# A gated MLP with seven-product block matmuls: sums of the down weights made in the first pass and kept in HBM, the other sums of the down stage on VectorE, fixed accumulator banks

## The chip, the cores and the metric

The kernel runs on one core of one Trainium2 chip. The metric is device time in microseconds (us) of that core, lower is better. The kernel before took 612.03 us (median of 4 runs, 611.32 to 613.72).

## The reference

```python
# x: 1 x 2048 x 1024, w_gate and w_up: 1024 x 3584, w_down: 3584 x 1024, all bf16
g = jnp.einsum("bsd,df->bsf", x, w_gate)
u = jnp.einsum("bsd,df->bsf", x, w_up)
h = jax.nn.gelu(g, approximate=True) * u
return jnp.einsum("bsf,fd->bsd", h, w_down)
```

## The kernel before

The kernel goes over x in two passes of 1024 rows. A pass has 14 "units" (gate and up for 256 columns of the hidden size, `u` = 0 to 13) and then one "down stage" (all of h times w_down). The first unit of the first pass is computed plainly while x is still being transposed, so units with seven products start at `u` = 1 there.

Every large product is cut into 2 x 2 blocks and computed with seven block products instead of eight. That saves one matmul in eight on TensorE and costs sums of blocks on the other engines: sums of weights ("s" in a unit, "t" in the down stage), sums of activations ("t" in a unit, "s" in the down stage), and additions of the seven products. A sum that goes into a matmul is written as fp32r, a 4-byte type.

```python
def dve(out, a, b, op):                       # L84
    nc.vector.tensor_tensor(out=out, in0=a, in1=b, op=op)
def pool(out, a, b, op):                      # L87
    nc.gpsimd.tensor_tensor(out=out, in0=a, in1=b, op=op)
def bank():                                   # 8 PSUM banks, handed out in turn
    return psum.tile([P, N], f32, name="bank")

def make_s(w):                                # sums of gate/up weights of one unit: 8 on GpSimd
    ...
    for i in range(2):
        s1.append(new(pool, a21, a22, ADD, "s1", sh))
    for i in range(2):
        s2.append(new(pool, s1[i], w[:, i, :KH, :P], SUB, "s2", sh))
    ...
def times(fb, c, g, u):                       # h = gelu(g) * u
    dve(hT[:, fb // NJ, fb % NJ, c, :], g, u, MUL)

def unit(u, xT, w, s, t, after_p5):
    ...                                       # seven products for gate (i=0) and up (i=1)
    c11 = [new(dve, c[i], p1[i], ADD, "sum", dtype=f32) for i in GU]
    ...
    times(2 * u, 0, gelu(c11[0]), c11[1])
    ...
    after_p5()                                # loads the next unit's weights, then make_s of them
    ...
    for i in GU:
        product(c[i], s4[i], tb, False)       # the product with s4 ("the fourth"): my mark
    ...
```

In the down stage the sums for products 5 and 6 (`prepare65`) and 7 and 3 (`prepare73`) are made just ahead of the matmuls that use them, for each of 14 values of `j`, partly on GpSimd:

```python
def prepare65(j):
    ra, rb = raw[j]                           # w_down, loaded again in each pass
    s1, t1, s2, t2 = q65[j] = pieces(j)
    dve(s1, hT[:, 0, j, 1, :], hT[:, 1, j, 1, :], ADD)
    pool(t1, ra[:, N:], ra[:, :N], SUB)
    dve(s2, s1, hT[:, 0, j, 0, :], SUB)
    dve(t2, rb[:, N:], t1, SUB)
    if j > 0:
        late4(j - 1)
    ...
def late4(j):
    eng = dve if j % 3 == 2 else pool
    q4[j] = new(eng, raw[j][1][:, :N], q65[j][3], SUB, "t4")
...
def prepare73(j):
    ...
    dve(s3, hT[:, 0, j, 0, :], hT[:, 0, j, 1, :], SUB)
    pool(t3, rr[:, 1, :], rr[:, 0, :], SUB)
    eng = pool if j % 2 == 1 else dve
    eng(sx, hT[:, 1, j, 0, :], hT[:, 1, j, 1, :], SUB)
    dve(s4, sx, s3, ADD)
...
def down(ip, last, next_x, next_ops):
    ...                                       # products 1 and 2 from plain h and w_down: 28 steps of 4 matmuls
    for i in I:                               # a finished quarter: added, cast, stored
        store(ip, 0, i, 0, lambda st: dve(st, c[i], p1[i], ADD))
    c = [bank() for _ in I]                   # the next accumulators: need those four to be out
    for t in range(NJ + LAG):
        ...                                   # products 6 and 5; then 3 and 7; then 4
```

So a down stage has 7 x 14 x 4 = 392 matmuls, and per `j` eight sums: `s1`, `s2`, `t1`, `t2`, `t4`, `s3`, `t3`, and `s4` with its helper `sx` (nine operations, 126 in a stage).

The start, in the order of the program: the first half of x is transposed on TensorE (`turn(xT, xn0, 0)`), then 32 plain matmuls, the weight sums for unit 1 (`make_s`), the second half of x (`turn(xT, xn1, 1)`), two products `times`, the 16 sums of x (`make_t`, all on VectorE), then 32 more plain matmuls and two more `times`.

## Time and profile before

| What, in the profiled run (span 610.5 us) | us |
|---|---|
| Start, up to the mark of unit 1 | 48.8 |
| Twelve units to the mark of unit 13 | 151.4 |
| First down stage (203.81 to 316.37) | 112.6 |
| Second down stage (497.36 to 607.20) | 109.8 |

Marks: I took the start of what I call the fourth product of a unit, the one with the weight sum `s4` (it is the sixth of the seven to run; in the trace, the group of matmuls that reads `tb` and `s`), since every unit has exactly one.

The page's slices: each digit is the busy share of one fortieth of the span in tenths, and PEclk is the granted TensorE clock in tenths.

```profile
PE   8659999999999994989698999999999999678977
...
DVE  1695665656555899998496766756566579999982
...
POOL 0956688877883467684446999888868437659640
PEclk9789999999999998899998999999999999969899
```

TensorE is at 9 except at the start (the first three digits) and in two stretches with lower digits, slices 16 to 22 and 35 to 40, which lie in the down stages and just behind the first. There VectorE shows mostly 8s and 9s, GpSimd is busy too, and the clock dips.

The stretch view of the two down stages (columns: stretch, length, then busy time and instructions of TensorE, TensorE's weight loads, VectorE, ScalarE and GpSimd; granted clock, DMA share, GB/s):

```profile
203.81:316.37 112.56, 94.53 (x390) 65.68 (x393) 100.06 (x107) 25.84 (x48) 67.10 (x46) 0.94 0.47 139
497.36:607.20 109.84, 93.99 (x390) 65.78 (x392) 95.42 (x97) 23.47 (x42) 65.26 (x43) 0.94 0.36 118
```

TensorE has 94.5 us of work in 112.6 us, some of that at a reduced clock. VectorE is busy for 100.1 us and GpSimd for 67.1 us at the same time. Memory is not what limits: the DMA engines are busy 47% of the time on average, and in this stage TensorE waits for no transfer. It idles 18.0 us: 8.9 for finished accumulators that VectorE has to store, 4.7 for sums of GpSimd and 4.1 for sums of VectorE.

In the timeline of TensorE the marks of units 2 and 3 are at 61.43 and 74.05 us: an undisturbed unit takes 12.62 us, and its matmuls follow each other without a wait. The units are bound by TensorE; there is little to gain there.

Why is VectorE so busy in the down stage? The timeline of VectorE in the first down stage of before (columns: start, length, engine, line, operation, tiles, shapes, count):

```profile
225.04 1.65 DVE L85 TENSOR_TENSOR q<-hT 128x512 fp32r<-128x512 bf16 x1
226.72 0.69 DVE L85 TENSOR_TENSOR q<-q,hT 128x512 fp32r<-128x512 f32 x1
227.33 0.68 DVE L85 TENSOR_TENSOR q<-raw,q 128x512 fp32r<-128x512 bf16 x1
...
228.54 1.65 DVE L85 TENSOR_TENSOR q<-hT 128x512 fp32r<-128x512 bf16 x1
230.22 1.53 DVE L85 TENSOR_TENSOR q<-q,hT 128x512 fp32r<-128x512 f32 x1
```

and the timeline of GpSimd in the same kernel and stretch:

```profile
222.97 3.18 POOL L88 TENSOR_TENSOR q<-raw 128x512 fp32r<-128x512 bf16 x2
228.10 1.54 POOL L88 TENSOR_TENSOR t<-raw,q 128x512 fp32r<-128x512 bf16 x1 [1.96 <-DVE q L85]
229.60 1.60 POOL L88 TENSOR_TENSOR q<-raw 128x512 fp32r<-128x512 bf16 x1
```

On VectorE, operations of the same shape take either 0.68 to 0.69 or 1.5 to 1.65 us. They are all sums of two operands in SBUF. GpSimd is in its own sums up to 226.15 and again from 228.10 to 231.20; the slow operations are the ones that fall into these times, and the fast ones fall between them. The Trainium skill states the reason (SBUF — State Buffer, "Who interferes with whom"): VectorE and GpSimd share one of their port pairs to SBUF, and "A DVE instruction with two SBUF inputs contends with a GpSimd instruction that reads SBUF, not with one that only writes it". The durations here agree with it: where GpSimd reads, a VectorE sum takes more than twice as long. The view of the tile `q` gives it for all sums of one form (minimum/median/maximum in ns):

```profile
L85 DVE TENSOR_TENSOR q<-hT x62: 674/1159/1658, 217.6 to 589.6; 128x512 fp32r<-128x512 bf16 x62
```

What this does to TensorE is seen in its timeline, where the bracket tells how long TensorE idled before the group and on whom it waited:

```profile
244.06 6.61 PE L106 MATMUL bank<-w 128*128 128x512 f32 x16 [8.94 <-DVE st L85]
250.51 11.72 PE L106 MATMUL bank<-q 128*128 128x512 f32 x51
```

TensorE waits 8.94 us until VectorE has added and stored four finished accumulators, since these additions stand in VectorE's queue behind slow sums. After the idle the next 16 matmuls take 6.61 us, 0.41 us each (the fp32r matmuls behind them start 0.227 us apart), at a granted clock of 0.50 in the stretch 240 to 250 us. The Trainium skill has this as well (TensorE: Matmul & The Clock Gate, "Part 1: The HAM clock gate"): the clock is halved after an idle window. So a wait costs more than its own length.

The start of before, in the timeline of TensorE:

```profile
45.48 3.48 PE L106 MATMUL bank<-t,s 128*128 128x512 f32 x8 [6.11 <-issue]
48.80 1.55 PE L106 MATMUL bank<-tb,s 128*128 128x512 f32 x6
```

Here there is a hole of 6.11 us inside unit 1. The trace names nobody that TensorE waited for (`issue`); I read the cause from what VectorE does. It is then working through the 16 sums of x, to 42.45 us; the first eleven of them take 1.3 to 1.66 us each, since GpSimd makes the weight sums at the same time.

### The profile page before, as it was taken

The page shows a single profiled execution, that of the slowest core. Times are in us where ns is not written, and L with a number is a line of the kernel's source. Part 1 is how long each engine was busy: PE and PEld are TensorE (multiplying, and loading weights), DVE is VectorE, ACT ScalarE, POOL GpSimd, SP SyncE. Part 2 cuts the span into 40 slices and gives each one's busy share as a digit, 9 for nine tenths or more (in the row PEclk, how much of TensorE's full clock was granted, in tenths as well). Part 3 has the DMA queues.
Part 4 walks back from the last instruction along what each step waited for, and adds up shares of the span by engine and source line. Part 5 has one row for each costly group of instructions (what it writes and reads, how often), then busy time and mean ns, then how long its engine had stood idle before and what let it go on. Part 6 is the DMA issues. An engine that isn't in the chain of part 4 may idle for free. (4 is left out here: it accounts for less than half of the span.)

```text
span 610.5 us, 7424 instructions
## 1 busy us (share of the span) xinstructions
PE 554.5 (91%) x2398; PEld 385.9 (63%) x2432; DVE 436.1 (71%) x501; ACT 248.4 (41%) x426; POOL 408.7 (67%) x312
## 2 busy tenths in 40 slices
PE   8659999999999994989698999999999999678977
PEld 4337766777667552867475777767777665366756
DVE  1695665656555899998496766756566579999982
ACT  2525555565555110141453555555555531003350
POOL 0956688877883467684446999888868437659640
PEclk9789999999999998899998999999999999969899
DMA  8354222342003951434446743222400196232312
GB/s 261 84 154 119 73 70 69 99 110 69 1 1 123 371 162 35 153 88 104 121 129 179 193 120 88 70 69 77 125 7 2 56 345 220 70 119 71 103 34 87
DMA packets 96133, 67.59 MB, mean 111 GB/s; under 512 B 12128, under 2 KB 87904, under 8 KB 96096
## 3 DMA queue, kind: packets, MB, share of 16 engines
q1 hardware_dynamic: 96096, 67.12, 37.5%
q8 instruction: 20, 0.33, 0.2%
q14 instruction: 17, 0.14, 0.1%
HBM read 60.82 MB, written 4.19 MB: 106 GB/s over the span
## 5 line engine op out<-in xcount | busy, mean ns | idle before, releaser
L88 POOL TENSOR_TENSOR s<-w 128x512 fp32r<-128x512 bf16 x108 | 137.6, 1293 | 90.1 <-PE bank L106 57.6
L106 PE MATMUL bank<-t,s 128*128 128x512 f32 x648 | 161.2, 404 | 8.7 <-issue 6.1
L106 PE MATMUL bank<-w 128*128 128x512 bf16 (+1 forms) x532 | 135.7, 401 | 26.2 <-DVE st L85 17.9
L85 DVE TENSOR_TENSOR sum<-bank,p 128x512 f32<-128x512 f32 x108 | 74.4, 691 | 103.3 <-PE bank L106 101.4
L106 PEld LDWEIGHTS bank<-t,s 128*128 128x128 f32 x648 | 123.4, 191 | 38.8 <-issue 7.6
L102 ACT COPY p<-bank 128x512 f32<-128x512 f32 x124 | 71.3, 589 | 80.5 <-PE bank L106 67.1
L85 DVE TENSOR_TENSOR hT<-g,sum 128x512 bf16<-128x512 f32 x81 | 82.6, 1020 | 12.9 <-ACT g L152 7.1
L88 POOL TENSOR_TENSOR q<-raw 128x512 fp32r<-128x512 bf16 x48 | 73.0, 1530 | 27.0 <-DMA raw<-in_w_down_dram 12.1
L152 ACT ACTIVATE g<-sum 128x512 f32<-128x512 f32 x81 | 51.2, 632 | 96.9 <-DVE sum L85 95.1
L106 PEld LDWEIGHTS <-w 128*128 128x128 bf16 x496 | 45.0, 99 | 68.0 <-issue 23.0
L106 PE MATMUL bank<-t,sa 128*128 128x512 f32 x328 | 84.1, 404 | 0.0
L106 PE MATMUL bank<-q 128*128 128x512 f32 x272 | 69.3, 401 | 15.1 <-DVE q L85 10.1
L88 POOL TENSOR_TENSOR s<-w,s 128x512 fp32r<-128x512 bf16 x54 | 74.8, 1404 | 0.0
L106 PEld LDWEIGHTS bank<-t,sa 128*128 128x128 f32 x328 | 61.7, 188 | 14.8
L85 DVE TENSOR_TENSOR q<-hT 128x512 fp32r<-128x512 bf16 x62 | 71.0, 1163 | 0.0
L106 PEld LDWEIGHTS bank<-q 128*128 128x128 f32 x272 | 50.6, 190 | 30.5 <-POOL q L88 16.5
L88 POOL TENSOR_TENSOR s<-s,w 128x512 fp32r<-128x512 f32 x54 | 65.4, 1230 | 0.0
L97 ACT CAST tb<-raw 128x512 fp32r<-128x512 bf16 x28 | 17.2, 625 | 115.1 <-PE bank L106 78.1
L106 PE MATMUL bank<-tb,s 128*128 128x512 f32 x216 | 53.3, 389 | 0.0
L106 PE MATMUL bank<-raw,hT 128*128 128x512 bf16 x218 | 49.4, 379 | 0.3
L106 PEld LDWEIGHTS bank<-tb,s 128*128 128x128 f32 x216 | 40.5, 188 | 8.5
L102 ACT COPY u<-bank 128x512 f32<-128x512 f32 x62 | 35.7, 588 | 18.0 <-PE bank L106 17.8
(43 smaller groups left out, 463.3 us busy)
## 6 DMA issues: line engine op xcount, KB each, us to landing
raw<-in_w_down_dram SPq DMA_DIRECT2D x112, 256.0 KB, 5.3
w<-in_w_gate_dram SPq DMA_DIRECT2D x27, 512.0 KB, 4.0
w<-in_w_up_dram SPq DMA_DIRECT2D x27, 512.0 KB, 5.3
out_dram<-st SPq DMA_DIRECT2D x32, 128.0 KB, 1.7
xn<-in_x_dram SPq DMA_DIRECT2D x8, 256.0 KB, 4.4
w<-in_w_gate_dram SPq DMA_DIRECT2D x4, 128.0 KB, 4.1
w<-in_w_up_dram SPq DMA_DIRECT2D x4, 128.0 KB, 4.2
w<-in_x_dram SPq DMA_TRANSPOSE x16, 2.9
```

What stands on the lines that cost most here:

```text
L85: nc.vector.tensor_tensor(out=out, in0=a, in1=b, op=op)
L88: nc.gpsimd.tensor_tensor(out=out, in0=a, in1=b, op=op)
L97: nc.scalar.copy(out=t, in_=src)
L102: nc.scalar.copy(out=t, in_=ps)
L106: nc.tensor.matmul(ps, lhsT=lhs, rhs=rhs, start=start, stop=stop, skip_group_check=True)
L152: nc.scalar.activation(g, src, ACT.Gelu_apprx_tanh)
```

## The change

The intent was to take GpSimd out of the down stages and to make the down stage's weight sums (`t1`, `t2`, `t4`, 42 operations) only once: VectorE makes them in the units of the first pass, where it has time, they go to HBM as fp32, and each down stage loads them. Of the sums that stay, all are on VectorE, and `s4` is now made from `s2`, without the helper `sx`: five sums per `j`, 70 in a stage. The accumulators get fixed banks. To have room, the kernel holds fewer weight tiles and loads the weights of a unit one unit earlier. The additions in a unit write one of their results in place in PSUM, so the product of `times` reads PSUM and not two SBUF operands. Not shown below: in the first down stage the loads of x for the next pass start at once, and the sums for that pass's first unit are made inside the stage, all on VectorE; the last four accumulators of a stage are copied out by ScalarE alone.

```diff
-    def bank():
-        return psum.tile([P, N], f32, name="bank")
+    bank = [psum.tile([P, N], f32, name=f"bank{i}") for i in range(8)]
+    even, odd, cc, dd = bank[0:2], bank[2:4], bank[4:6], bank[6:8]
 ...
-    def make_s(w):
+    def make_s(w, eng):                 # unit 1 and unit 0 of pass 2: dve; all others: pool
 ...
+        def add(ps, other):
+            g = new(dve, ps[0], other[0], ADD, "sum", dtype=f32)
+            dve(ps[1], ps[1], other[1], ADD)
+            return g, ps[1]
 ...
+    td = dpool.tile([P, NJ, 3, N], f32, name="td")         # in HBM
+    def keep(j, part):                                      # called in a unit of the first pass
+        ra, rb = wraw[j]
+        if part == 0:
+            made[j] = mpool.tile([P, 3, N], f32r, name="m") # a single buffer
+            dve(made[j][:, 0], ra[:, N:], ra[:, :N], SUB)
+        elif part == 1:
+            dve(made[j][:, 1], rb[:, N:], made[j][:, 0], SUB)
+        else:
+            dve(made[j][:, 2], rb[:, :N], made[j][:, 1], SUB)
+    def store_made(j):
+        nc.sync.dma_start(out=td[:, j], in_=made[j].bitcast(f32))
 ...
+    def make12(j):                                          # for prepare65
+        dve(s1, hT[:, 0, j, 1, :], hT[:, 1, j, 1, :], ADD)
+        dve(s2, s1, hT[:, 0, j, 0, :], SUB)
 ...
+    def make73(j):                                          # for prepare73
+        dve(s3, hT[:, 0, j, 0, :], hT[:, 0, j, 1, :], SUB)
+        dve(t3, rr[:, 1, :], rr[:, 0, :], SUB)
+        dve(s4, hT[:, 1, j, 0, :], s12[j][1], SUB)
 ...
-    s = make_s(w)
+    s = make_s(w, dve)                                      # the start
     turn(xT, xn1, 1)
 ...
-    ps = [bank() for _ in JI]
+    ps = bank[0:2] + bank[6:8]
 ...
+    def making(u):                                          # which j in which unit
+        return {1: [0], 2: [1, 2], 3: [3], 4: [4, 5]}.get(u, [u + 1] if 4 < u < NU - 1 else [])
+    fetch_wd(0)
+    ahead = load_w(2)
 ...
             def prepare():
-                    nxt["w"] = load_w(u + 1)
-                    nxt["s"] = make_s(nxt["w"])
+                nxt["w"], nxt["s"] = ahead, None
+                if u + 1 < NU:
+                    nxt["s"] = make_s(ahead, pool)
+                if u + 2 < NU:
+                    ahead = load_w(u + 2)
```

## The prediction

> **What bounds it now.** The stretch view gives TensorE 150.2 of 150.9 us busy in gate/up units 2 to 13 of the first pass, 12.61 us a unit in the timeline: TensorE-bound. Losses are elsewhere:
>
> - Start: unit 1 ends at 52.9 us. TensorE waits 5.3 us for transposed x and 6.1 us in unit 1, for sums slowed to 1.6 us.
> - First down stage: 203.8 to 316.4, 112.6 us. At the undisturbed rates of the timeline (0.213 us per bf16, 0.227 to 0.233 per fp32r matmul) its 392 matmuls need about 88.5.
> - First unit of pass 2: 18.6 instead of 12.6 us.
> - Second down stage: 497.4 to 607.2, 109.8 us.
>
> In the down stages VectorE is 95 to 99% busy for 65 us, and TensorE's largest wait (8.9 us each) is for four stores queued behind VectorE's sums. A VectorE sum of two SBUF operands takes 0.68 us alone but 1.5 to 1.65 beside a GpSimd sum; GpSimd's go from 1.13 to 1.6. The Trainium skill (SBUF — State Buffer, "Who interferes with whom") says that a two-input VectorE instruction contends with GpSimd's reads; the trace agrees. Two engines blocking each other bound the stage. The idle also costs clock: the 16 matmuls after it take 0.41 us each.
>
> **What the change does.**
> 1. Down stage: GpSimd's 40-odd sums go away; VectorE keeps 70 sums and 8 stores, 78 x 0.68 = 53 us of 88.
> 2. Weight sums, once: 42 VectorE operations in pass 1, three per unit, six in units 2 and 4, 0.7 to 1.6 us each. VectorE's load goes from about 7.5 to 10.5 of 12.6 us per unit (products now read PSUM: 0.68 instead of 1.02 us). Single units hide it; double ones stall 1 to 2 us each.
> 3. DMA: 11 MB written once; each down stage reads 11 MB of fp32 sums for 7.3 MB of raw bf16. Its first 28 steps (24 us) move as much as before (370 to 399 GB/s in the trace), but the first stage also gets the 16 x transposes there, about 10 us of engine time: 0 to 4 us of TensorE wait.
> 4. Start: unit 1's sums at 0.62 us on VectorE; x copies 1 us later; no 6.1 us hole, no cold restart.
> 5. Fixed banks: no cost.
>
> **Sum.** Start -8; pass-1 units +4; first down stage -20 (to 92.5); first unit of pass 2 -5; second down stage -18.5 (to 91). Together -47.5: 612 becomes **565 us**, 8 in 10 between **555 and 583**. Chances: faster by over 2% 0.95, within 2% 0.04, slower 0.01.
>
> **What would show each step right.** Unit 2 starts near 45 us. Units stay at 12.6 us, but up to 14.5 in units 2 to 5. In the down stages VectorE sums average under 0.75 us, VectorE is busy under 75%, GpSimd idle; no TensorE wait over 3 us; granted clock 0.97 or more; 89 to 95 us each. TensorE busy about 97%.
>
> **What would make it wrong.** (a) Down stages DMA-bound: TensorE waiting for w_down or stored sums, DMA share near 1 beyond the first 25 us, worse in the first. (b) The 52 slots run out (28 held by sums of h), loads issue late and the in-order queue stalls. (c) Pass-1 sums delay the PSUM sums: units of 13 us or more throughout. (d) VectorE waits for the single buffer of finished sums to reach HBM. Each would cost 5 to 20 us.

## The result

The kernel after took 560.05 us (median of 4 runs, 559.93 to 560.38), against 612.03 for before over its four runs. The ratio is 0.9148, with a 95% interval of 0.9129 to 0.9167. Ratios here are the mean time of one kernel's runs over that of the other's of the same rounds, so they are not quite the ratio of the medians. The mean granted clock went from 0.964 to 0.990. All outputs are right.

With the marks of the two traces, the 51.9 us between the spans (610.5 and 558.6) split into the terms of the prediction:

| Term | Before | After | Difference | Predicted |
|---|---|---|---|---|
| Start to the mark of unit 1 | 48.80 | 46.27 | -2.5 | -8 |
| Unit 1 to unit 13 of pass 1 | 151.38 | 152.50 | +1.1 | +4 |
| First down stage | 112.56 | 87.74 | -24.8 | -20 |
| Rest, up to the mark of unit 0 of pass 2 | 16.99 | 12.98 | -4.0 | -5 |
| Unit 0 to unit 13 of pass 2 | 164.00 | 163.54 | -0.5 | 0 |
| From there to the end (second down stage) | 116.77 | 95.57 | -21.2 | -18.5 |

The slices of the page of after:

```profile
PE   5969999999999999999999999999999999999997
...
DVE  1797978788777778388695545555545548757730
...
POOL 0433596998788100000048766677777700000000
PEclk9998999999999999999999999999999999999999
```

TensorE's only low digits are now at the start (and the last slice, where the kernel ends). GpSimd is all but idle in the down stages, and the clock is at 9 from the fifth slice on. The stretch view of the two down stages of after:

```profile
202.40:290.14 87.74, 87.58 (x390) 63.29 (x393) 67.60 (x106) 26.15 (x47) 3.33 (x3) 1.00 0.86 247
466.66:555.25 88.59, 88.22 (x390) 63.24 (x392) 52.38 (x84) 24.01 (x43) 0.00 (x0) 1.00 0.56 183
```

TensorE is busy for 87.58 of 87.74 us and 88.22 of 88.59 us, at full clock. The DMA share in the first stage is 0.86, because the stored sums and the transposed x come in together, but TensorE doesn't wait for them. VectorE's busy time fell from 100.1 to 67.6 and from 95.4 to 52.4 us. In the first stage that includes the 24 sums for the next pass's first unit, which is why the count there is 106.

VectorE's timeline in the first down stage of after, where the same group of four stores is found as in the wait of before:

```profile
227.61 2.48 DVE L90 TENSOR_TENSOR st<-bank,p 128x512 bf16<-128x512 f32 x4 [5.53 <-PE bank L111]
230.01 0.68 DVE L90 TENSOR_TENSOR q<-hT 128x512 fp32r<-128x512 bf16 x1
...
232.98 0.68 DVE L90 TENSOR_TENSOR q<-hT,q 128x512 fp32r<-128x512 bf16 x1
```

The four stores (2.48 us) now start when TensorE is done: VectorE waits 5.53 us for TensorE, and not the other way round. Every sum that the stage needs takes 0.68 or 0.69 us (two sums of the next pass's x, at its end, take 1.65 beside GpSimd). The view of the tile `q` for the form shown of before:

```profile
L90 DVE TENSOR_TENSOR q<-hT x56: 680/686/694, 203.3 to 525.5; 128x512 fp32r<-128x512 bf16 x56
```

The one large term that failed is the start. The timeline of TensorE in after:

```profile
11.96 0.95 PE L399 MATMUL bank<-ident,xn 128*128 128x128 bf16 x8 [4.79 <-DMA xn<-in_x_dram]
...
14.93 7.36 PE L111 MATMUL bank<-xT,w 128*128 128x512 bf16 x31
...
40.99 5.45 PE L111 MATMUL bank<-t,s 128*128 128x512 f32 x12 [4.41 <-DVE hT L90]
46.27 2.02 PE L111 MATMUL bank<-tb,s 128*128 128x512 f32 x8
```

There are a wait of 4.79 us for x at 11.96, before the first plain matmul, and a wait of 4.41 us for `hT` at 40.99. The matmuls after the second one run at 0.45 us each, at a granted clock of 0.50 (40.99 to 46.27). In VectorE's timeline the wait is explained:

```profile
31.22 1.65 DVE L90 TENSOR_TENSOR t<-xT,xT 128x512 fp32r<-128x512 bf16 x1
32.90 0.69 DVE L90 TENSOR_TENSOR t<-xT,t 128x512 fp32r<-128x512 bf16 x1
...
37.24 2.49 DVE L90 TENSOR_TENSOR t<-xT,t 128x512 fp32r<-128x512 bf16 x4
39.65 1.28 DVE L90 TENSOR_TENSOR hT<-g,bank 128x512 bf16<-128x512 f32 x2
```

The last two products of the start (39.65, `hT<-g,bank`, which free banks 6 and 7 for unit 1) stand behind all 16 sums of x, and the first five of these (25.12 to 32.87) take 1.48 to 1.65 us and not 0.69. GpSimd's timeline tells what ran beside them:

```profile
20.91 2.91 POOL L93 TENSOR_TENSOR s<-w 128x512 fp32r<-128x512 bf16 x2 [19.61 <-DMA w<-in_w_gate_dram]
...
29.14 3.18 POOL L93 TENSOR_TENSOR s<-w,s 128x512 fp32r<-128x512 bf16 x2
```

These are the weight sums of unit 2, from 20.91 to 32.32 us. In before they came from 26.33 to 38.89, behind those of unit 1. The change took unit 1's sums off GpSimd, and unit 2's, with their weights now loaded a unit earlier, moved up into the gap.

### The profile page after: what moved, and what is told of

Same layout as the page of the kernel before. It is cut to its first block, busy times and chain, and to the rows that moved or that the text cites. A ratio compares the mean times of both kernels' runs of the same rounds, so it can differ in the third digit from the quotient of the medians.

```text
span 558.6 us, 7422 instructions
## 1 busy us (share of the span) xinstructions
PE 541.4 (97%) x2398; PEld 381.1 (68%) x2432; DVE 367.7 (66%) x533; ACT 247.5 (44%) x430; POOL 242.6 (43%) x206
## 4 chain that ended last, share of the span: by engine, by line
PE 89%; DMA 4%; DVE 4%; issue 1%; ACT 1%; SPq 0%; DVEq 0%; ACTq 0%
PE bank L111 88%; DMA td<-m 2%; DVE m L90 2%; DMA xn<-in_x_dram 2%; DVE hT L90 1%; DVE t L90 1%; ACT g L157 0%; DVE sum L90 0%; PE bank L399 0%; SPq L391 0%; DVE xT L402 0%; ACT sa L102 0%; ACT st L362 0%; ACT u L107 0%; SPq L411 0%
## 5 line engine op out<-in xcount | busy, mean ns | idle before, releaser
L93 POOL TENSOR_TENSOR s<-w 128x512 fp32r<-128x512 bf16 x100 | 122.7, 1246 | 203.5 <-DVE t L90 103.0
L111 PE MATMUL bank<-xT,w 128*128 128x512 bf16 x468 | 111.6, 380 | 2.1 <-DVE xT L402 0.2
L90 DVE TENSOR_TENSOR hT<-g,bank 128x512 bf16<-128x512 f32 x112 | 76.7, 687 | 18.6 <-PE bank L111 8.5
L90 DVE TENSOR_TENSOR sum<-bank,p 128x512 f32<-128x512 f32 x54 | 37.2, 688 | 72.4 <-PE bank L111 72.3
L93 POOL TENSOR_TENSOR s<-w,s 128x512 fp32r<-128x512 bf16 x50 | 61.8, 1260 | 0.0
L111 PE MATMUL bank<-q 128*128 128x512 f32 x240 | 59.1, 389 | 0.0
L111 PE MATMUL bank<-t,sa 128*128 128x512 f32 x216 | 58.6, 413 | 0.0
L111 PEld LDWEIGHTS bank<-t,sa 128*128 128x128 f32 x216 | 40.7, 188 | 10.5
L90 DVE TENSOR_TENSOR q<-hT 128x512 fp32r<-128x512 bf16 x56 | 38.4, 687 | 10.3 <-PE bank L111 9.1
L90 DVE TENSOR_TENSOR bank<-bank,p 128x512 f32<-128x512 f32 x54 | 37.6, 696 | 8.3 <-PE bank L111 6.9
```

The source lines that it names most:

```text
L111: nc.tensor.matmul(ps, lhsT=lhs, rhs=rhs, start=start, stop=stop, skip_group_check=True)
```

## The experiments

Three theories of the large gain were open after this:

- A (mine): two engines collide. VectorE's sums of two SBUF operands and GpSimd's sums block each other. Taking GpSimd's sums out of the down stage is the gain.
- B: fewer sums. The sums of weights are made once and `sx` is saved; collisions matter little.
- C: the fixed banks. Order or hand-over of accumulators was what made TensorE wait.

And two theories of the missing part at the start: D, the collision of GpSimd's early unit-2 sums with the sums of x; and E, the order of TensorE's instructions (the wait for x at 11.96). The order of the instructions shows that the scheduler put 24 of the 32 transposes of the second half of x ahead of the first plain matmul in after, and behind it in before.

Each kernel ran four times (the last one five), beside before on the same chip. The groups of runs that share a chip are e1 to e4 (before: 612.99), e5 to e8 (613.42) and e9 to e12 (614.28).

### e1_all_vector: before, with all sums of the down stage on VectorE

```diff
-        pool(t1, ra[:, N:], ra[:, :N], SUB)
+        dve(t1, ra[:, N:], ra[:, :N], SUB)
 ...
-        eng = dve if j % 3 == 2 else pool
+        eng = dve                                  # late4: t4
 ...
-        pool(t3, rr[:, 1, :], rr[:, 0, :], SUB)
-        eng = pool if j % 2 == 1 else dve
+        dve(t3, rr[:, 1, :], rr[:, 0, :], SUB)
+        eng = dve                                  # sx
```

> The kernel before with the GpSimd sums of the down stage moved to VectorE and nothing else; VectorE then does 126 sums and 12 stores per down stage where it did about 85 and 12. Theory (the two engines block each other): its two-operand sums fall from a mean of about 1.1 us to 0.68, one every 0.61 us, and each down stage gets some 10 us shorter in spite of the added sums: 585 to 603 us in all; the wait for the four stores stays near 9 to 12 us. Rival (the number of sums binds, not the collisions): 126 sums at the old 1.1 us fill about 139 us, and the time rises above 640 us.

Measured: 583.83 us, ratio 0.952 (0.9474 to 0.9566). VectorE now does all 126 sums of a stage, nothing is saved, and the kernel is 29 us faster. The view of the tile `q` in this kernel, and the stretch view of the first 378 recorded matmuls of its first down stage:

```profile
L85 DVE TENSOR_TENSOR q<-hT x76: 679/685/689, 215.9 to 560.0; 128x512 fp32r<-128x512 bf16 x76
```

```profile
203.57:297.60 94.03, 89.12 (x378) 62.18 (x381) 91.28 (x150) 24.12 (x44) 0.00 (x0) 0.96 0.56 163
```

The sums, these and those of the other forms, are all at 0.68 to 0.70 us. The stage, up to the next pass's first matmul at 300.47, takes 96.9 us instead of 112.6. Over the whole stage VectorE's instructions went up from 107 to 153, and their busy time went down from 100.1 to 94.2 us. One part of what I expected missed: I thought that the 8.9 us waits for the stores would stay, because VectorE would be 97% busy. They are gone; the largest waits of TensorE on VectorE in this kernel are 1.4 us. That is theory A without any saving, and it gives more than half of the whole gain (29 of 52 us). The remaining 24 us belong to the rest of the change. By the marks of the two profiled runs (578.8 and 558.6 us), 15.9 of the 20.2 us between them lie in the two down stages, where VectorE is still busy for 97% of the stretch in this kernel. That taking sums off VectorE gives these 15.9 us is likely but not shown alone, since the loads and the order of the stage change too.

### e2_banks_only: before, with the fixed banks of after

```diff
-    def bank():
-        return psum.tile([P, N], f32, name="bank")
+    bank = [psum.tile([P, N], f32, name=f"bank{i}") for i in range(8)]
+    even, odd, cc, dd = bank[0:2], bank[2:4], bank[4:6], bank[6:8]
 ...
-        e = [bank(), bank()]
+        e, c, d = banks                            # in unit; likewise in down, turn and the start
```

> The kernel before with fixed accumulator banks and nothing else. Theory: the 8.9 us waits for the four stores come from the stores standing behind VectorE's sums, not from how banks are handed out, so both waits remain and the down stages stay at 110 to 113 us; the instruction order shows 24 transposes of the second half of x moved ahead of the first plain products on TensorE, so the first plain products start near 15 us instead of 8.3, and the total is 610 to 622 us. Rival (fixed banks take the waits away): the two waits vanish and the time falls to about 590 us.

Measured: 613.7 us, ratio 1.0016 (0.9976 to 1.0056), the same. The two waits of 8.9 us stay. Theory C falls. This kernel also has the transposes moved ahead, as after has, so that order comes with the fixed banks; why the scheduler does it then was not looked into further.

### e3_dummy_sums: after, with 42 useless GpSimd sums in each down stage

```diff
     def make12(j):
         s1, s2 = s12[j] = [slot([P, N], f32r, "q") for _ in range(2)]
+        for _ in range(3):
+            pool(warm, hT[:, 0, j, 1, :], hT[:, 1, j, 1, :], ADD)
```

> The changed kernel with 42 useless GpSimd sums per down stage, two SBUF operands each, into an unused tile. VectorE's work, the loads and the banks are unchanged. Theory (collisions): while they run VectorE's two-operand sums rise from 0.68 to a mean of 1.3 us or more, 28 of them no longer fit into the 24 us of the first two products, TensorE waits again for the stores, and the time rises by 15 to 50 us over the 560 us of the changed kernel. Rival (GpSimd was slow only with its own work, and its sums were late): the dummy sums harm nothing, 559 to 562 us.

Nobody uses what these sums write, so they add no dependence that the stage needs. Measured: 592.57 us, ratio 0.9668 (0.9624 to 0.9713), 32 us slower than after. GpSimd has nothing else to do there and runs the first stage's sums in one go, from 194.58 to 245.31, across the part of the stage ahead of the four stores. Beside them VectorE's sums take 1.5 to 1.65 us again (and 0.68 from 248.17 on), and TensorE again waits for the four stores. From VectorE's timeline, then TensorE's:

```profile
222.48 1.53 DVE L90 TENSOR_TENSOR q<-q,hT 128x512 fp32r<-128x512 f32 x1
223.94 1.64 DVE L90 TENSOR_TENSOR q<-hT 128x512 fp32r<-128x512 bf16 x1
```

```profile
246.51 5.39 PE L111 MATMUL bank<-w,q 128*128 128x512 f32 x16 [13.42 <-DVE st L90]
```

A wait of 13.42 us, and 14.1 us in the second stage; together 27.5 of the 32 us. Most of the rest is the slower clock after each wait: the 16 matmuls behind the two waits take 5.39 and 6.29 us, 0.34 and 0.39 us each where 0.23 is usual, about 4.4 us more. VectorE's own work is that of after. Theory B can't explain this; A does.

### e4_dummy_memset: after, with 84 GpSimd writes in each down stage

```diff
     def make12(j):
         s1, s2 = s12[j] = [slot([P, N], f32r, "q") for _ in range(2)]
+        for _ in range(6):
+            nc.gpsimd.memset(warm, 0.0)
```

> The same with 84 GpSimd memsets per down stage in place of the 42 sums: GpSimd is busy but reads nothing. Theory, with the Trainium skill (SBUF — State Buffer, Who interferes with whom): an instruction that only writes does not collide with a two-input VectorE sum, so the sums stay at 0.68 us and the time at 559 to 562 us. Rival (any GpSimd work at the same time slows VectorE): as with the dummy sums, in proportion to the time in which GpSimd is busy.

Measured: 559.69 us, ratio 0.9135 (0.91 to 0.917), no different from after. The groups view of this kernel (count, then busy time and mean ns):

```profile
L257 POOL MEMSET warm<- 128x512 bf16 x168 | 88.1, 524 | 9.6
```

GpSimd is busy with them for 44 us per stage, and the sums that VectorE makes meanwhile stay at 0.68 to 0.69 us. So it is not GpSimd being busy that costs, but GpSimd reading SBUF. This is what the sentence of the Trainium skill quoted above says, and here it is measured.

### e5_each_pass: after, with the weight sums made and stored in both passes

```diff
-            js = making(u) if ip == 0 else []
+            js = making(u)
 ...
-                for j in making(u + 1) if ip == 0 else []:
+                for j in making(u + 1):
 ...
-            if ip == 0 and making(u - 1):
+            if u > 0 and making(u - 1):
```

> The changed kernel, but the sums of the down weights are made in the gate/up units of both passes and stored twice, so nothing is made once. Theory: what matters is that they are out of the down stage; in a unit VectorE has room. In the changed kernel the first pass's units lost about 1 us against before (152.5 for 151.4 us), so the second pass loses about 1 us too: 560.5 to 563 us. Rival (having half as many of these sums gives the gain): 5 us slower or more.

Measured: 561.6 us, ratio 0.916 (0.9111 to 0.9208), 1.5 us over after, which is inside the noise (the intervals overlap). Making the sums once is not the gain; having them made outside the down stage is. In the units VectorE has the time.

### e6_back28: after, with 28 of the 70 sums of a stage back on GpSimd

```diff
-        dve(s3, hT[:, 0, j, 0, :], hT[:, 0, j, 1, :], SUB)
-        dve(t3, rr[:, 1, :], rr[:, 0, :], SUB)
+        pool(s3, hT[:, 0, j, 0, :], hT[:, 0, j, 1, :], SUB)
+        pool(t3, rr[:, 1, :], rr[:, 0, :], SUB)
```

> The changed kernel with 28 of the 70 sums of each down stage (the difference of h and the difference of w_down of the third product) back on GpSimd. Theory: collisions stretch VectorE's 14 remaining sums there and GpSimd's 28 take 1.2 to 1.6 us each, about 40 us in a window of about 45, so the slack nearly closes: 560 to 568 us, VectorE sums near 1 us in the second half of the stage. Rival (all sums must be on VectorE for any of the gain): over 575 us.

Measured: 566.0 us, ratio 0.9232 (0.9183 to 0.9281), 6 us over after. The view of the tile `q` shows the collisions:

```profile
L90 DVE TENSOR_TENSOR q<-hT,q x28: 681/1572/1651, 228.9 to 528.8; 128x512 fp32r<-128x512 bf16 x28
```

The sums collide (median 1572 ns) but TensorE hardly waits in the stages: they take 88.4 and 89.8 us, and the only waits in them are 1.5 us for stored sums, in the second. VectorE is busy for 72% of the first stage and 51% of the second here (73.4 us of 202 to 304, 47.3 of 468 to 560), so there is slack for it. By the marks, 3.3 of the 4.7 us between the profiled spans (563.3 and 558.6) lie behind the first stage, up to the mark of unit 0 of pass 2, where TensorE waits 2.02 us for ScalarE at 299.36; 1.3 lie between the last mark and the end. So a collision costs TensorE little where VectorE has slack: from 227.8 to 290 us of this kernel, where nearly all of the first stage's collisions fall, VectorE is busy for 68%. Before's VectorE was busy for 89% of the first stage, and for 99% of its first 40 us. Load and place were not varied apart: nearly all of GpSimd's sums here fall behind the four stores, and those of e3 ahead of them.

### e7_start_pool and e12_start_pool2: after, with GpSimd's unit-2 sums held back

```diff
             def prepare():
                 nonlocal ahead
                 nxt["w"], nxt["s"] = ahead, None
+                if ip == 0 and u == 1:
+                    pool(warm, t[3][KH - 1], t[3][KH - 1], ADD)
```

One small GpSimd sum reads the last sum of x, so everything behind it in GpSimd's queue has to wait until VectorE is done with the sums of x. e12 is the same kernel run again in the last group.

> The changed kernel with one small GpSimd sum that reads the last of VectorE's sums of x, ahead of GpSimd's weight sums for unit 2, which therefore start only after them. Theory: at the start GpSimd's sums for unit 2, now loaded a unit early, collide with VectorE's 16 sums of x (six of them at 1.5 to 1.65 us); without that the last one ends near 35 instead of 39.7 us, the two products behind it end near 36, TensorE's 4.4 us wait falls below 1 us, and the time is 554 to 557 us. Rival (the wait comes from something else in the start): no change, 559.5 to 561.

> The kernel with only GpSimd's weight sums for unit 2 held back, again, to be compared with the fully ordered start on the same chip: 552.5 to 554 us, as before.

Measured: e7 553.27 us, ratio 0.9019 (0.8969 to 0.9069); e12 553.56 us, ratio 0.9005 (0.8984 to 0.9025). That is 6.5 to 7 us faster than after. From e7's timelines of VectorE, GpSimd and TensorE:

```profile
33.87 1.28 DVE L90 TENSOR_TENSOR hT<-g,bank 128x512 bf16<-128x512 f32 x2
```

```profile
34.12 1.04 POOL L93 TENSOR_TENSOR warm<-t 128x512 bf16<-128x512 f32 x1 [32.81 <-DVE t L90]
```

```profile
36.95 2.11 PE L111 MATMUL bank<-t,s 128*128 128x512 f32 x8 [0.46 <-ACT u L107]
38.90 1.99 PE L111 MATMUL bank<-tb,s 128*128 128x512 f32 x8
```

The sums of x all take 0.69 us or less and end at 33.96 us, and not at 39.73, the wait for `hT` is gone (0.46 us are left, for ScalarE), and the mark of unit 1 is at 38.90 instead of 46.27. (In after's trace five sums of x are slow, not the six of the expectation.) The wait for x is still there (3.96 us at 11.46). Theory D is shown, and the 7.4 us gained at the mark are more than the 5.5 us that the prediction had missed at the start.

### e10_start_order: after, with the transposes of the second half of x back behind the plain matmuls

```diff
-    turn(xT, xn1, 1)
+    with tc.issue_after(held["mm"].ins):       # held["mm"]: the last plain matmul of the first half
+        turn(xT, xn1, 1)
```

> The changed kernel with only the TensorE order restored: the transposes of the second half of x behind the first plain products. Theory: the first products start near 8.5 instead of 15 us, but the copies of the second half of x stand behind the weight sums on VectorE until near 23 us, so the time saved turns into a wait there: 559 to 561 us. Rival (the moved transposes cost their 6 us): 553 to 556.

Measured: 560.01 us, ratio 0.9108 (0.9087 to 0.9129), the same as after. TensorE's timeline in this kernel:

```profile
7.40 7.07 PE L111 MATMUL bank<-xT,w 128*128 128x512 bf16 x32 [1.10 <-ACT xT L404]
...
21.01 12.38 PE L111 MATMUL bank<-xT,w 128*128 128x512 bf16 x48 [4.76 <-ACT g L157]
...
41.40 4.66 PE L111 MATMUL bank<-t,s 128*128 128x512 f32 x12 [4.40 <-DVE hT L90]
```

The first plain matmul starts at 7.40 and not at 14.93 us, but the time is given back: a wait of 4.76 us has appeared at 21.01, for ScalarE's gelu, which stands in its queue behind casts of unit 1's weights. VectorE's queue, which sets the pace here, hardly moved: its copies of the second half of x stand behind the sums of unit 1's weights, at 22.17 as against 22.73 us in after, and the products that TensorE waits for come at 40.07 as against 39.65. Theory E falls: the wait at 11.96 is visible and costs nothing as long as VectorE's queue sets the pace.

### e11_start_times: after, with two of the products moved ahead of the last four sums of x

```diff
-    t = make_t(xT)
     ps = bank[0:2] + bank[6:8]
-    for p, (j, i) in zip(ps, JI):
-        plain(p, i, j, 1, range(NKB))
-    for j in range(2):
-        times(j, 1, gelu(ps[2 * j]), ps[2 * j + 1])
+    def between():                              # called in make_t ahead of the four t4
+        for p, (j, i) in zip(ps, JI):
+            plain(p, i, j, 1, range(NKB))
+        for j in range(2):
+            times(j, 1, gelu(ps[2 * j]), ps[2 * j + 1])
+    t = make_t(xT, between)
```

> The changed kernel with only the two products of the second plain set moved ahead of the last four sums of x, GpSimd's collisions left as they are. Theory: TensorE waits in unit 1 for these products, through the fixed banks; they come four sums (2.4 us) earlier, so the time is 557 to 558.5 us. Rival (the wait is for the sums of x themselves): 559.5 to 561.

Measured: 559.24 us, ratio 0.9092 (0.9066 to 0.9119). That is under 1 us better than after, less than I expected, and I call it inconclusive. TensorE resumes at 39.02 and not at 41.40 us, but its fourth product starts at 45.97, as against 45.89 in e10: unit 1's first additions on VectorE come at 41.29 all the same, behind the last sums of x, and TensorE's next products need what follows from them.

### e8_start_all: e7, e10 and e11 together

The edits of the three together; the copies of the transposes are also placed ahead of the weight sums of unit 1:

```diff
+    with tc.issue_after(held["mm"].ins):
+        turn(xT, xn1, 1)
     s = make_s(w, dve)
-    turn(xT, xn1, 1)
 ...
+    t = make_t(xT, between)                     # as in e11
 ...
+                if ip == 0 and u == 1:          # as in e7
+                    pool(warm, t[3][KH - 1], t[3][KH - 1], ADD)
```

> The changed kernel with the start put in order: transposes of the second half of x held behind the first plain products on TensorE, their copies ahead of the weight sums on VectorE, the two products ahead of the last four sums of x, and GpSimd's sums for unit 2 behind all of them. Theory: the first plain products start near 8.5 us, the second near 18 instead of 24, the fourth product of unit 1 starts near 38 instead of 46.3 us: 550 to 554 us. Rival (the loads at the start bind): no better than 557.

Measured: 553.29 us, ratio 0.9016 (0.8973 to 0.9059), no better than e7 alone. TensorE starts its plain matmuls at 8.35 but waits 3.74 us for `hT` at 32.47, since the products now stand behind 12 sums of x, and the mark of unit 1 is at 39.97.

### e9_start_best: e8, with the products after the first four sums of x and the last four sums in unit 1

```diff
             t2.append(new(dve, b22, t1[k], SUB, "t2"))
+            if k == 1:
+                between()
 ...
+        def rest():
+            for k in range(KH):
+                t4.append(new(dve, xT[0][:, KH + k], t2[k], SUB, "t4"))
 ...                                            # in unit 1, after its first additions:
+        held.pop("rest", lambda: None)()
```

> The start of the previous run (everything in order) with two more moves on VectorE: the two products that free the second pair of banks come after four of the sums of x instead of after twelve, and the last four sums of x come after unit 1's first sums of products. Theory: in the previous run TensorE waited 3.7 us for those two products although their operands were ready near 25 us; without that the fourth product of unit 1 starts near 36 us instead of 40.0, and the time is 549 to 551.5 us, 2 us or more below the run with only GpSimd held back. Rival (the start is bound by the count of VectorE's sums, wherever they stand): no better than 552.5.

Measured: 554.47 us, ratio 0.9015 (0.8994 to 0.9035), against 553.56 for e12 in the same group. The mark of unit 1 came to 35.90 us, as I had meant, 2.6 us ahead of e12. But the time, which I had expected at 549 to 551.5, didn't fall. TensorE's timeline of this kernel in units 2 and 3:

```profile
48.37 1.98 PE L111 MATMUL bank<-tb,s 128*128 128x512 f32 x8
...
53.88 2.11 PE L111 MATMUL bank<-t,sa 128*128 128x512 f32 x8 [1.57 <-DVE sum L90]
...
57.70 3.88 PE L111 MATMUL bank<-t,s 128*128 128x512 f32 x16 [0.82 <-POOL s L93]
...
64.38 1.98 PE L111 MATMUL bank<-tb,s 128*128 128x512 f32 x8
```

From the mark of unit 2 to that of unit 3 are 16.0 us; in e12 they are 12.0 (51.88 to 63.87). The gain is lost to three waits, for VectorE, GpSimd and, at 62.48, ScalarE (0.90 us). VectorE's new sums of down weights in unit 2 had waited 3.17 us for the single buffer `m` to be stored, and then took 1.45 us, and 3.09 for the next two, beside GpSimd's sums of unit weights. When TensorE is ready sooner, the next limit is the other engines' work that the change has put there.

## Why the prediction was right or wrong

**The time was right.** 565 us was predicted, 560.05 measured, inside the range of 555 to 583, and "faster by over 2%" holds. That it came so near is in part luck: the start gave 5.5 us less and the first unit of pass 2 1 us less than the sum had, while the two stages gave 4.8 and 2.7 us more and the units of pass 1 cost 2.9 us less.

**The mechanism of the down stages was right.** The prediction said that two engines blocking each other bound the stage. e1 (same sums, all on one engine: -29 us), e3 (useless sums that read: +32 us) and e4 (useless writes: 0) show it. e2 and e5 take out the rivals: the banks, and making the sums once.

**Their size was too small.** I gave 92.5 and 91 us to the two stages (-20 and -18.5); they took 87.7 and 88.6 (-24.8 and -21.2). The 88.5 us that I had worked out for 392 undisturbed matmuls was about right (in the trace 112 bf16 matmuls at 0.216 us and 280 fp32r ones at 0.227 make 87.8 us), and the 2.5 to 4 us that I added for DMA waits were not needed: TensorE's waits for the stored sums in the first stage are 0, in spite of a DMA share of 0.86. I predicted VectorE under 75% busy; it was 77% in the first stage (67.6 of 87.7 us) and 59% in the second. The 24 sums for the next unit explain the first, and I had counted 8 stores where VectorE has 12.

**Pass-1 units: +4 predicted, +1.1 measured.** The units 2 to 5 of after take 13.41, 11.99, 13.37 and 12.73 us between marks, but a changed order of the matmuls moves the marks: in sum they are 51.5 against 50.47 us. The only stall that TensorE's timeline shows there is 0.48 us. VectorE's new sums do collide with GpSimd's weight sums in the units (first of each three: median 1.45 us), but the units have the slack for it: VectorE is busy for 9.8 us of a unit of about 12.5, where before had 7.6 and the prediction 10.5. The warning (d) did come true in itself, without harm: VectorE waited 16.6 us in 11 times for the single buffer of finished sums, but TensorE didn't have to.

**First unit of pass 2: -5 predicted, -4.0 measured.** No experiment took this term apart.

**The step that failed is item 4, "Start: unit 1's sums at 0.62 us on VectorE; x copies 1 us later; no 6.1 us hole, no cold restart", with its term "Start -8".** It measured -2.5. Unit 1 was to be over near 45 us, and its last product ends near 52.6. The hole did not go away; it became one of 4.4 us on `hT`, with a cold restart behind it. I had looked at what the change takes from GpSimd at the start (unit 1's sums) and not at what stands next in GpSimd's queue: the sums of unit 2, which moved from 26.33 up to 20.91 us and ran beside the sums of x in the place of unit 1's. It is the very collision that the prediction names as the limit of the down stages, half taken away and half left. The first sum of x started 2.7 us later than in before (25.12 against 22.46), behind VectorE's copies of x, which came 6.8 us later and not 1 (22.73 against 15.89); with five slow sums in place of eleven the last one ended 2.7 us sooner (39.73 against 42.45), and the mark came 2.5 us sooner. e7 takes it away with one dependence and gets 7 us back. The second thing that the traces showed at the start, the moved transposes with a wait of 4.79 us, looked the more striking and is worth nothing (e10).

**What points further.** e12 (and e7) beat both kernels: 553.56 against 614.28 us for before in the same group. The start isn't exhausted, but e8 and e9 gained nothing over them by a further change of VectorE's order, and e9 lost its lead in units 2 and 3. Whether spreading GpSimd's and VectorE's sums over those units would keep it was not tried.

## What to carry to other kernels

Two engines that share a port to SBUF are not two engines: here a VectorE sum of two SBUF operands took more than twice its time when GpSimd read beside it. First try to put all the work on one of them, even if the count of that one goes up. When a change takes work off an engine, look at what stands next in that engine's queue: it moves up into the gap, and may collide there just as well. The largest wait in a timeline can be worth nothing when another queue sets the pace, so take it away alone once before believing in it.

## What the Trainium skill lacked or had wrong

- SBUF — State Buffer ("Who interferes with whom") is right about who collides, and e4 agrees with its exception for operations that only write. It gives no durations for colliding sums of two tensors. Here a VectorE sum of two 128x512 operands goes from 0.68 or 0.69 to 1.5 to 1.65 us beside GpSimd's sums. GpSimd's own, of the same form, go from 1.15 us (before, at 17.64) to 1.59 us (before, at 26.33).
- The same page ("Summary: rules for kernel authors") says that the second one to issue fully blocks until the first finishes. The trace shows operations that last longer, not waiting ones: the lost time is inside the duration of the instruction (1.65 us), so in a profile the engine looks busy. The page doesn't say that it has to be looked for there. Nor do the times fit two sums that simply follow one another: from 26.3 to 38.9 us in before, sums of VectorE start every 1.55 us and sums of GpSimd every 1.56, where alone they start every 0.60 and 1.11 us, 1.71 together.
- TensorE: Matmul & The Clock Gate ("Back-to-back issue gap") gives about 131 ns per matmul at N = 512 as the sustained rate, and about 216 ns for an isolated one. In these traces bf16 matmuls at full clock, in a long stream, start 0.216 us apart (e10: 32 from 7.40, 7.07 us in all), at the isolated figure; I saw 131 ns nowhere.
- I found no rate for fp32r matmuls there. The traces show 0.227 us at 512 columns: before's 56 matmuls from 303.66 to 316.37, 12.71 us.
